# Loading K and R of the first four units two tokens to a partition

## The chip, the core and the metric

The kernel runs on one core of a Trainium2 chip. The metric is the device time of one execution in microseconds (us); the figure used for comparisons is the median of several executions. Engines are named as the profile names them: PE is the matmul side of TensorE, PEld its weight loads, DVE is VectorE, ACT is ScalarE, POOL is GpSimd, SP is SyncE (SPq is SP's queue of DMA issues).

## What is computed

An RWKV-5 attention is followed by a two-layer block. The attention has batch 4, 8 heads, 768 tokens, 48 elements a head:

```python
for t in range(S):
    kt, vt, rt = k[:, :, t], v[:, :, t], r[:, :, t]
    cur = np.einsum('bhd,bhe->bhde', u[None] * kt, vt)
    y[:, :, t] = np.einsum('bhd,bhde->bhe', rt, state + cur)
    state = w[None, :, :, None] * state + np.einsum('bhd,bhe->bhde', kt, vt)
```

The result, as x with 3072 tokens of 384 elements, goes through `h = x @ w_in` (384 to 2048), the SmeLU with beta 1 (0 below -1, h above 1, and (h + 1)**2 / 4 between), and `g @ w_out` (2048 to 384). Inputs and output are float32.

## The kernel before

**Units.** The attention is done in chunks of 128 tokens. One batch and one chunk make a unit: 24 units, numbered chunk by chunk over the four batches, so units 0 to 3 (U0 to U3) are the first chunk of the four batches and carry no state from before. Two units make a pair m (256 tokens), which is the tile of the two-layer block.

**A unit's steps** (function `attention`, lines 469 to 674). K, R and V of a unit are loaded as float32 tiles of 128 tokens x 8 heads x 48 (line 427: every token and head is one run of 192 bytes, 192 KB a load). K is multiplied by w to the power -(t+1), `Winv` (line 483), R by w to the power t, `Wpow` (line 487), where t is the token's place in the chunk; both products go as bf16 into one tile KR, each head padded from 48 to 64. TensorE transposes KR in eight blocks, two heads each (line 505), a copy brings them from PSUM to SBUF as RK (line 508; helper at line 318). Matmuls of RK with itself give the 128x128 matrices A of each head (line 535); they are masked to the strict triangle (lines 550 and 553, AT; for a few units after a cast `am` at line 546). The diagonal comes from the product P of the two halves of RK and a matmul with u (lines 565 and 571, copied as dg). Matmuls of AT with V (line 609), and from the second chunk on of RK with the state Tbd (line 606), give y; VD (line 596) is added to it (line 621) to give x. TensorE transposes x for the first six units (line 631) and a DMA does for the others (line 639), into xTa. For the state, KR's K half is the stationary operand of matmuls with V (line 657); T is updated and scaled (lines 664 to 668) and copied as bf16 into Tbd (line 672). From unit 10 on a DMA transposes KR (line 524). The squares of x at line 647 feed only a check of range at the end.

**The two-layer block.** Layer one of a pair has eight groups of six matmuls (line 715), each evicted by ACT as a square (line 730, g). The PSUM pool "h" has two slots, so a group waits for the eviction of the group two before it. Layer two of a unit has four groups of four matmuls (line 749), each of which needs one quarter of w_out. The weights come as float32 in four loads of w_in (I0 to I3) and four of w_out (O0 to O3), 768 KB each, in runs of 2048 and 1536 bytes (line 454), and are cast to bf16 by DVE, ACT and POOL (line 318).

**What sets the order.** All instructions are listed as operations with engines, dependencies, slots of pools and due times, and a planner (`Plan.run`, line 98) places them one by one with costs of its own; every engine then executes its own list in that order. The due times come from `CFG` (`due`, `step`, `bias`) and, for the early loads, from `CFG["order"]` (lines 433 to 437). All loads go through SP's queue, in one order, with at most eight DMAs under way at a time. A load also waits until a slot of its pool is free; the weights' float32 tiles have the five slots of "wf". TensorE fills its time up to a set point with dummy matmuls of zeros (line 403).

Of the kernel before, what the change touches and what calls it, by code (L numbers as in the profile page):

```python
# [9 lines left out]
F32 = mybir.dt.float32  # L10
BF16 = mybir.dt.bfloat16
AF = mybir.ActivationFunctionType
# [2 lines left out]

SEM = 0.06
CFG = {
    "order": "U0 U1 U2 U3 I0 I1 I2 I3 O0 O1 O2 U4 U5 O3 U6 U7",
    "tpe": 10,
    "dmm": 8,  # L20
    "xpe": 6,
    "pair": 4,
    "cold": 9.0,
    "fine": 0,
    "am0": 2,
    "am1": 0,
    "norm": 100.0,
    "wide": 0,
    "due": [32.65, 38.55, 28.55, 31.54, 45.68],
    "step": 9.83,  # L30
    "warm": 24.0,
    "steady": 45.0,
    "slack": 0,
    "split": 2,
    "bias": {
        "P": 2.76, "am": -14.26, "at": -12.0, "bd": -7.97, "cI": 4.41, "cO": 11.29, "c_uw": 4.37, "dc": 5.73,
        "dg": 7.99, "ku": -5.64, "kw": 7.93, "ldK": -0.11, "ldR": 0.75, "ldVf": 1.96, "mask": -7.09, "red": 3.59,
        "rk": -1.31, "rkk": 0.04, "rkr": 5.61, "rw": -4.62, "st": 7.95, "t": -0.44, "tr": 0.61, "trd": -2.94,
        "trk": -6.22, "trr": 1.71, "tw": -8.79, "v": 0.76, "vd": -0.65, "x": 1.06, "x2": 1.39, "xp": -2.11,
        "xt": 0.98, "xtd": -1.36, "y": -5.96,  # L40
    },
}

# [151 lines left out]
def pe(t):  # L195
    return {"PE": (t, t + 0.17)}
# [22 lines left out]
def kernel(  # L219
# [30 lines left out]
    while len(D_m) < NB + 2:  # L250
# [8 lines left out]
    slots = {  # L259
        "a": 4, "h": 2, "o": 2,  # L260
        "K": 6, "R": 6, "Vf": 6, "wf": 5, "KR": 4, "KU": 3, "V": 6, "RK": 4, "AT": 3, "P": 2, "VD": 3, "dg": 3,
        "x": 5, "x2": 2, "g": 5, "os": 3, "sq": 1, "ss": 2, "am": 2,
    }
    P = Plan(slots)
    rows = rot.tile([1, 2, H, DP], F32, name="rows", tag=f"g_{slots['g'] - 1}")
    lw = rot.tile([128, H, D], F32, name="lw", tag="x2_1")

    def get(b, shape, dtype):
        pl = psum if b.pool in ("a", "h", "o") else rot
        nm = f"{b.pool}_{b.slot}"  # L270
        b.t = pl.tile(shape, dtype, name=nm, tag=nm)
        return b.t
# [19 lines left out]
    i_int = const.tile([128, 1], mybir.dt.int32, name="i_int")  # L292
    i_col = const.tile([128, 1], F32, name="i_col")
    negj_col = const.tile([128, 1], F32, name="negj_col")
    Wpow = const.tile([128, H, D], F32, name="Wpow")
    Winv = const.tile([128, H, D], F32, name="Winv")
    uw = const.tile([128, NP, 2], BF16, name="uw")
# [19 lines left out]
    def copy(eng, o, i):  # L317
        (nc.scalar.copy if eng == "ACT" else V_ENG[eng].tensor_copy)(o, i)  # L318

    def pair(t, p):  # L320
        return t[:, 2 * p : 2 * p + 2, :].rearrange("q h d -> q (h d)")
# [3 lines left out]
        return bass.AP(tensor=src.tensor, offset=src.offset, ap=[[0, 1], [1, H * D]])  # L325

    heads = lambda t: t.rearrange("p (h d) -> p h d", h=H)
    c_wr = P.op("c_wr", {"SP": (0.5, 0)}, lambda e: nc.sync.dma_start(out=w_sp[0:128:64, :], in_=w.rearrange("(s h) d -> s (h d)", s=2)), due=-1000, dma=(0.05, 1, 0.5))  # L328
    c_ubc = P.op("c_ubc", {"SP": (0.4, 0)}, lambda e: nc.sync.dma_start(out=u_bc, in_=row_bcast(u)), due=D_m[CFG["dmm"] // UB] - 25, dma=(0.7, 8, 0.6))
    c_cols = P.op("c_col", {"POOL": (0.2, 0.2)}, lambda e: nc.gpsimd.iota(i_int, pattern=[[0, 1]], base=0, channel_multiplier=1), due=-100)  # L330

    def f_kr(i):
        def fn(e):
            nc.vector.memset(KR[i], 0.0)
        return fn

    kr0 = [P.op(f"c_kr{i}", {"DVE": (0.48, 0.5)}, f_kr(i), due=-90 + i) for i in range(slots["KR"])]

    def f_col(e):
        nc.vector.tensor_copy(i_col, i_int)  # L340
        nc.vector.tensor_scalar(negj_col, i_col, -1.0, -1.0, ALU.mult, ALU.add)
    c_icol = P.op("c_icol", {"DVE": (0.3, 0.35)}, f_col, deps=[c_cols], due=-92)
    c_ident = P.op("c_ident", {"POOL": (0.6, 0.7)}, lambda e: make_identity(nc, ident), due=-98)

    def f_um(e):
# [26 lines left out]
        for s in range(2):  # L372
            nc.scalar.activation(lw[:, lws[s]], wbb[s].t, AF.Ln)
    c_lw = P.op("c_lw", {"ACT": (0.58, 0.65)}, f_lw, deps=[c_wb], uses=wbb, due=-98)
    c_winv = P.op("c_winv", {"ACT": (0.5, 0.58)}, lambda e: nc.scalar.activation(Winv, lw, AF.Exp, scale=negj_col), deps=[c_lw, c_icol], due=-97)  # L375
    c_wpow = P.op("c_wpow", {"ACT": (0.5, 0.58)}, lambda e: nc.scalar.activation(Wpow, lw, AF.Exp, scale=i_col), deps=[c_lw, c_icol], due=-96)
    c_lrow = P.op("c_lrow", act(384, False), lambda e: nc.scalar.copy(rows[:, 0, :, 0:D], lw[0:1]), deps=[c_lw, c_rz], due=8.2)

    c_ur = P.op("c_ur", {"ACT": (0.4, 0)}, lambda e: nc.scalar.dma_start(out=rows[:, 1, :, 0:D], in_=heads(row(u))), deps=[c_rz], due=-99.5, dma=(0.05, 1, 0.6))
# [32 lines left out]

    loads = {}

    def add_load(i):
        b, c = units[i]
        t0 = c * C
        res = {}  # L420
        due = LD[i]
        for j, (nm, src) in enumerate((("K", k), ("R", r), ("Vf", v))):
            bf = Buf(nm)

            def fn(e, bf=bf, src=src):
                t = get(bf, [128, H, D], F32)
                nc.sync.dma_start(out=t, in_=src[b, :, t0 : t0 + C, :].rearrange("h s d -> s h d"))  # L427

            o = P.op(f"ld{nm}{i}", {"SP": (0.5, 0)}, fn, after=[loads[i - 1][nm][1] if i else None], allocs=[bf], due=due + 0.1 * j, dma=(1.08, 64, 0.6))
            res[nm] = (bf, o)  # L430
        loads[i] = res

# [10 lines left out]
    for tag, q in [(x[0], int(x[1:])) for x in ORDER if x[0] in "IO"]:  # L443
# [8 lines left out]
        def fn(e, bf=bf, src=src, shape=shape):  # L452
            t = get(bf, shape, F32)
            nc.sync.dma_start(out=t, in_=src)  # L454
# [14 lines left out]
    def attention(i):  # L469
# [4 lines left out]
        by_pe, by_mm, x_pe = i < CFG["tpe"], i < CFG["dmm"], i < CFG["xpe"]  # L474
        D0 = D_m[m] + 1.5 * j
        (Kb, Ko), (Rb, Ro), (Vb, Vo) = loads[i]["K"], loads[i]["R"], loads[i]["Vf"]
        krb, vb, rkb, atb, yb, xb = Buf("KR"), Buf("V"), Buf("RK"), Buf("AT"), Buf(A), Buf("x")
        both = {**pool(384), "DVE": (0.51, 0.56)}
        prev = state.get(b)

        def f_kw(e):
            krb.t = KR[krb.slot]
            V_ENG[e].tensor_mul(krb.t[:, H:, 0:D], Kb.t, Winv)  # L483
        o_kw = P.op(f"kw{i}", both, f_kw, deps=[Ko, c_winv] + kr0, uses=[Kb], allocs=[krb], due=D0 - 6)

        def f_rw(e):
            V_ENG[e].tensor_mul(krb.t[:, :H, 0:D], Rb.t, Wpow)  # L487
        o_rw = P.op(f"rw{i}", both if soft else {"DVE": both["DVE"]}, f_rw, deps=[Ro, c_wpow, o_kw], uses=[Rb, krb], due=D0 - 5.8)

        def f_v(e):  # L490
            get(vb, [128, H, D], BF16)
            copy(e, vb.t, Vb.t)
        o_v = P.op(f"v{i}", {**act(384, False), **({**dve(384, True), **pool(384, False)} if soft else {})}, f_v, deps=[Vo], uses=[Vb], allocs=[vb], due=D0 - 4)

        if by_pe:
            trb = Buf(A)

            fine = i < CFG["split"]

            def f_tr(e, part):  # L500
                if trb.t is None:
                    get(trb, [128, 2 * NP, 128], BF16)
                    get(rkb, [128, 2 * NP, 128], BF16)
                for p in part:
                    nc.tensor.transpose(trb.t[:, p, :], pair(krb.t, p), ident)  # L505

            def f_rk(e, part):
                copy(e, rkb.t[:, part], trb.t[:, part])

            kp, rp = slice(NP, 2 * NP), slice(0, NP)  # L510
            half = {**act(512), **dve(512, True)}
            if fine:
                o_trk = P.op(f"trk{i}", pe(0.22), lambda e: f_tr(e, range(NP, 2 * NP)), deps=[o_kw, c_ident], uses=[krb], allocs=[trb, rkb], due=D0 - 5)
                o_trr = P.op(f"trr{i}", pe(0.22), lambda e: f_tr(e, range(NP)), deps=[o_rw], uses=[krb, trb, rkb], after=[o_trk], due=D0 - 4.8)
                o_rk1 = P.op(f"rkk{i}", half, lambda e: f_rk(e, kp), deps=[o_trk], uses=[trb, rkb], due=D0 - 4.2)
                o_rk2 = P.op(f"rkr{i}", half, lambda e: f_rk(e, rp), deps=[o_trr], uses=[trb, rkb], due=D0 - 4)
                o_rk = [o_rk1, o_rk2]
            else:
                o_tr = P.op(f"tr{i}", pe(0.44), lambda e: f_tr(e, list(range(NP, 2 * NP)) + list(range(NP))), deps=[o_kw, o_rw, c_ident], uses=[krb], allocs=[trb, rkb], due=D0 - 4.8)
                o_rk = [P.op(f"rk{i}", {**act(1024), **dve(1024, True)}, lambda e: copy(e, rkb.t, trb.t), deps=[o_tr], uses=[trb, rkb], due=D0 - 4)]  # L520
        else:
            def f_trd(e):
                get(rkb, [128, 2 * NP, 128], BF16)
                nc.sync.dma_start_transpose(out=rkb.t, in_=krb.t.rearrange("p h d -> p (h d)"))
            o_rk = [P.op(f"trd{i}", {"SP": (1.35, 0)}, f_trd, deps=[o_kw, o_rw], uses=[krb], allocs=[rkb], due=D0 - 9, dma=(1.45, 64, 0.0))]
# [124 lines left out]
        if c < NCH - 1:  # L650
            stb = Buf(A)
            DS = D_m[m + 2] + 1.5 * j

            def f_st(e):
                get(stb, [128, NP, 2 * D], F32)
                for p in range(NP):
                    mm(stb.t[:, p, :], pair(krb.t[:, H:, :], p), pair(vb.t, p), start=True, stop=True)  # L657
            o_st = P.op(f"st{i}", pe(0.17), f_st, deps=[o_kw, o_v], uses=[krb, vb], allocs=[stb], due=D0 - 0.2 if c else DS - 10)

            def f_t(e):  # L660
                for s in range(2):
# [235 lines left out]
```

## Time and profile before

| what | value |
|---|---|
| median of 8 executions | 179.17 us (178.07 to 182.0) |
| the profiled execution | 180.63 us, of which the span of its instructions 178.9 us |
| mean granted TensorE clock | 0.984 |
| busy in the span: PE, DVE, ACT, POOL | 168.4, 111.8, 121.2, 99.3 us |
| layer one, 576 matmuls | 273 ns each, 77.0 us |
| layer two, 400 matmuls | 323 ns each, 77.1 us |
| dummy matmuls | 47, 10.9 us |

The profile is one execution, taken by the hardware profiler. Times in its views count from the first instruction. The chain of work that ended last is followed back from the last instruction: at each step to what released it, or to the instruction before it on its engine. Busy times of matmuls overlap by their pipelining (273 ns each, while a group of six follows the one before it by 0.65 us in the timeline), so sums of busy time on PE are above the time that passes.

### The profile page before, as it was taken

To read this page: it belongs to the slowest core of one execution; us is meant where nothing else is said; L and a number is where in the kernel's file an instruction comes from. 1 tells how busy PE (TensorE), PEld (TensorE's weight loads), DVE (VectorE), ACT (ScalarE), POOL (GpSimd) and SP (SyncE) were. 2 spreads that over 40 slices of the span, in tenths; PEclk is the share of its full clock that TensorE was granted. 3 is DMA by queue.
4 is the path that set the end of the run, shared out by engine and by line. 5 is a ranking of instruction groups with operands and counts; after the bars stand their busy time and mean duration, and the time that the engine had idled before them with its cause. 6 is when DMAs were issued, how large, how long until landed. Compare 5 with 4: busy or idle time off the path is not lost.

```text
span 178.9 us, 4529 instructions
## 1 busy us (share of the span) xinstructions
PE 168.4 (94%) x1719; PEld 127.7 (71%) x1719; DVE 111.8 (63%) x220; ACT 121.2 (68%) x267; POOL 99.3 (56%) x138
## 2 busy tenths in 40 slices
PE   7999888959999999999999999999999999999990
PEld 4777676846777777777777777777777868777770
DVE  5599895496797898948862786697674817010000
ACT  4665777784768959559775597894896864755520
POOL 8234463126769697956776359599797941300000
PEclk9999999996999999999999999999999999999997
DMA  4999999797994999899699997998989863311111
GB/s 83 190 190 344 344 377 315 150 251 153 238 198 103 195 207 188 178 159 220 118 196 174 207 211 136 196 212 156 192 154 199 169 146 93 88 51 44 46 44 49
DMA packets 104717, 31.14 MB, mean 174 GB/s; under 512 B 97778, under 2 KB 103156, under 8 KB 104692
## 3 DMA queue, kind: packets, MB, share of 16 engines
q1 hardware_dynamic: 104676, 30.81, 80.4%
q8 instruction: 14, 0.23, 0.6%
q14 instruction: 11, 0.09, 0.2%
q10 hardware_dynamic: 16, 0.00, 0.0%
HBM read 20.65 MB, written 4.72 MB: 142 GB/s over the span
## 4 chain that ended last, share of the span: by engine, by line
PE 75%; DMA 11%; SPq 7%; issue 3%; POOL 1%; ACT 0%; POOLq 0%
PE o L749 35%; PE h L715 30%; DMA wf<-in_moe_w_out_dram 6%; SPq L427 5%; DMA wf<-in_moe_w_in_dram 5%; PE a L535 3%; PE a L609 2%; PE a L606 2%; PE a L657 2%; POOL w_out_sb L318 1%; PE a L505 1%; SPq L454 1%; SPq L328 0%; PE a L631 0%; ACT os L318 0%
## 5 line engine op out<-in xcount | busy, mean ns | idle before, releaser
L749 PE MATMUL o<-w_out_sb,g 128*128 128x384 bf16 (+2 forms) x400 | 77.1, 323 | 1.5 <-POOL w_out_sb L318 1.0
L715 PE MATMUL h<-xTa,w_in_sb 128*128 128x256 bf16 x576 | 77.0, 273 | 0.2 <-ACT w_in_sb L318 0.2
L730 ACT ACTIVATE g<-h 128x512 bf16<-128x512 f32 x96 | 56.6, 595 | 29.5 <-PE h L715 28.4
L715 PEld LDWEIGHTS <-w_in_sb 128*128 128x128 bf16 x576 | 54.6, 98 | 13.6 <-ACT w_in_sb L318 0.5
L749 PEld LDWEIGHTS <-g 128*128 128x128 bf16 x400 | 37.3, 98 | 17.6 <-issue 2.3
L553 DVE TENSOR_TENSOR AT<-a,umask 128x512 bf16<-128x512 f32 x46 | 29.0, 684 | 10.0 <-PE a L535 9.9
L596 POOL TENSOR_TENSOR VD<-V,dg 128x384 f32<-128x384 bf16 x18 | 15.9, 883 | 13.4 <-ACT V L318 4.0
L586 POOL TENSOR_TENSOR KU<-KU,R 128x384 f32<-128x384 f32 x16 | 17.3, 1082 | 4.0 <-DMA R<-in_r_dram 2.9
L487 DVE TENSOR_TENSOR KR<-R,Wpow 128x384 bf16<-128x384 f32 x22 | 16.0, 729 | 3.0 <-DMA R<-in_r_dram 2.7
L585 POOL TENSOR_TENSOR KU<-K,u_bc 128x384 f32<-128x384 f32 x16 | 17.6, 1101 | 0.0
L621 DVE TENSOR_TENSOR x<-a,VD 128x384 bf16<-128x384 f32 x24 | 13.1, 553 | 4.8 <-PE a L609 4.2
L318 ACT CAST Tbd<-T 48x192 bf16<-48x192 f32 x38 | 13.2, 348 | 3.6 <-POOL T L668 2.5
L668 POOL TENSOR_TENSOR T<-T,wc 128x192 f32<-128x192 f32 x20 | 11.4, 572 | 7.1 <-DVE T L664 3.6
L483 DVE TENSOR_TENSOR KR<-K,Winv 128x384 bf16<-128x384 f32 x16 | 12.4, 777 | 3.0 <-ACT Winv L375 1.6
L318 ACT COPY os<-o 128x384 f32<-128x384 f32 (+2 forms) x21 | 9.7, 463 | 6.2 <-PE o L749 5.1
L647 ACT ACTIVATE x<-x 128x384 bf16<-128x384 bf16 x24 | 12.4, 518 | 1.5 <-DVE x L621 1.0
L664 DVE TENSOR_TENSOR T<-T,a 48x192 f32<-48x192 f32 x32 | 11.2, 349 | 3.1 <-PE a L657 2.5
L403 PE MATMUL o<-zero 128*128 128x256 bf16 x47 | 10.9, 369 | 1.1 <-DVE zero L356 1.1
L318 ACT CAST V<-Vf 128x384 bf16<-128x384 f32 x20 | 10.1, 507 | 2.0 <-DMA Vf<-in_v_dram 1.8
L591 DVE TENSOR_REDUCE dg<-KU 128x8 f32<-128x384 f32 x16 | 8.7, 546 | 4.1 <-POOL KU L586 3.9
L800 POOL TENSOR_TENSOR ss<-sq 128x256 bf16<-128x256 bf16 x8 | 6.3, 789 | 8.3 <-ACT sq L791 8.3
L483 POOL TENSOR_TENSOR KR<-K,Winv 128x384 bf16<-128x384 f32 x8 | 8.2, 1028 | 2.5 <-DMA K<-in_k_dram 2.5
(83 smaller groups left out, 169.4 us busy)
## 6 DMA issues: line engine op xcount, KB each, us to landing
K<-in_k_dram SPq DMA_DIRECT2D x24, 192.0 KB, 4.1
R<-in_r_dram SPq DMA_DIRECT2D x24, 192.0 KB, 3.8
Vf<-in_v_dram SPq DMA_DIRECT2D x24, 192.0 KB, 4.2
out_dram<-os SPq DMA_DIRECT2D x19, 192.0 KB, 3.0
wf<-in_moe_w_in_dram SPq DMA_DIRECT2D x4, 768.0 KB, 8.0
wf<-in_moe_w_out_dram SPq DMA_DIRECT2D x4, 768.0 KB, 10.1
out_dram<-os SPq DMA_DIRECT2D x8, 96.0 KB, 2.2
xTa<-x SPq DMA_TRANSPOSE x18, 2.5
```

The source lines that it names most:

```text
L318: (nc.scalar.copy if eng == "ACT" else V_ENG[eng].tensor_copy)(o, i)
L483: V_ENG[e].tensor_mul(krb.t[:, H:, 0:D], Kb.t, Winv)
L487: V_ENG[e].tensor_mul(krb.t[:, :H, 0:D], Rb.t, Wpow)
L553: nc.vector.tensor_mul(atb.t[s], at_p[s].t, umask4)
L585: nc.gpsimd.tensor_mul(kub.t, Kb.t, u3)
L586: nc.gpsimd.tensor_mul(kub.t, kub.t, Rb.t)
L596: V_ENG[e].tensor_mul(vdb.t, vb.t, dgb.t[:, :, None].to_broadcast([128, H, D]))
L621: nc.vector.tensor_add(xb.t, yb.t[:, 0:384].rearrange("p (h d) -> p h d", h=H), vdb.t)
L647: nc.scalar.activation(x2b.t, xb.t.rearrange("p h d -> p (h d)"), AF.Square, accum_out=xn[:, i : i + 1])
L715: mm(hb.t[:, f, :], w_in_sb[:, kk, c * 128 : (c + 1) * 128], xT[m][:, kk, cols], start=(kk == 0), stop=(kk == nKb - 1))
L730: nc.scalar.activation(gb[m].t[:, 2 * n : 2 * n + 2, :], hb.t, AF.Square, bias=0.5, scale=0.5)
L749: mm(ob.t[:, : hi - lo], gb[m].t[:, f, j * C : (j + 1) * C], w_out_sb[:, f, lo:hi], start=(f == 0), stop=(f == nN - 1))
```

## The change

K and R of units 0 to 3 are loaded into a tile for each pair of units, in a slot of the pool "wf": unit 0 of the pair takes partitions 0 to 63, unit 1 takes 64 to 127, and every partition holds two neighbouring tokens, so a run is 384 bytes. There are four loads for a pair, of 64 partitions and 192 KB each. V is loaded as before. The multiplies then work on even tokens (z = 0) and odd tokens (z = 1) of both units at once, with four tables W2 in place of Winv and Wpow (four more exps on ACT); Winv and Wpow remain for the units after. TensorE transposes them, eight blocks for K and eight for R of a pair, and the copies from PSUM to RK write every second column, which puts the tokens in order again. The K half, which the state's matmuls need with tokens on partitions, is transposed back from RK by TensorE (four blocks a unit) and copied to a tile KB. The KR tiles are cleared only in their padding. Beside that the planner's settings differ (order of loads, due times, biases; x of units 6 and 7 transposed by TensorE; the am cast for unit 2 too; A matmuls of both units in one operation from pair 3 on; no split of unit 0's and 1's transposes), and the order of the instructions of every engine is planned anew.

```diff
-    "order": "U0 U1 U2 U3 I0 I1 I2 I3 O0 O1 O2 U4 U5 O3 U6 U7",
+    "order": "U0 U1 U2 U3 I0 I1 I2 I3 O0 O1 U4 O2 O3 U5 U6 U7",
-    "xpe": 6,
-    "pair": 4,
+    "xpe": 8,
+    "pair": 3,
+    "duo": 2,
-    "am0": 2,
+    "am0": 3,
-    "due": [32.65, 38.55, 28.55, 31.54, 45.68],
-    "step": 9.83,
+    "due": [8.31, 25.74, 32.52, 37.4, 41.83],
+    "step": 9.95,
-    "slack": 0,
-    "split": 2,
+    "slack": 0.19,
+    "split": 0,
...
+    c_w2 = []
+    for q in range(4):
+        c_w2.append(P.op(
+            f"c_wd{q}", {"ACT": (0.5, 0.58)}, lambda e, q=q: nc.scalar.activation(W2[:, q], lw, AF.Exp, scale=i2_col[:, q : q + 1]),
+            deps=[c_lw, c_icol], due=-97 + 0.1 * q,
+        ))
...
+        if i < UB * CFG["duo"]:
+            if i % UB == 0:
+                bf = Buf("wf")
...
+                            nc.sync.dma_start(out=bf.t[x * DP : (x + 1) * DP, j], in_=src[b, :, t0 : t0 + C, :].rearrange("h (i s) d -> i h (s d)", s=2))
...
+                        src = dd["D"].t[:, q].rearrange("p h (s d) -> p h s d", s=2)[:, :, z]
+                        V_ENG[e].tensor_mul(kb.t[:, H - q * H : 2 * H - q * H, 0:D], src, W2[:, 2 * q + z])
...
+                            nc.tensor.transpose(tb.t[:, z, p, :], pair(dd["kr"][z].t, NP - q * NP + p), ident)
...
+                dst = rkb.t[:, NP - q * NP : 2 * NP - q * NP, :].rearrange("a p (i s) -> a s p i", s=2)
+                copy(e, dst, dd["tr"][q].t[:, :, :, j * DP : (j + 1) * DP])
...
+                        nc.tensor.transpose(kbp.t[:, p, :], rkb.t[:, NP + p, :], ident)
...
+                    copy(e, kbb.t.rearrange("q h d -> q (h d)"), kbp.t.rearrange("q p d -> q (p d)"))
```

## The prediction

> **What bounds the kernel now.** First the chain of work that ended last, in order of time:
>
> ```profile
> 13.74 8.24 DMA wf<-in_moe_w_in_dram
> 21.98 11.11 DMA wf<-in_moe_w_out_dram
> ...
> 33.14 0.70 POOL w_out_sb L318
> 33.83 5.09 issue
> ...
> 38.94 1.35 POOL w_out_sb L318 x2
> ...
> 40.33 1.44 PE o L749 x4
> ```
>
> Columns: start, us, what. Up to 38.9 the end hangs on transfers; from 40.33 on it is TensorE's. The group at 40.33 is the fourth of layer two (I call it L2#4), the first to need O3, the last quarter of w_out. The 5.09 of "issue" at POOL is POOL waiting for O3: it was issued at 32.97 (timeline of SP's queue), took 5.9 to land (view of line 454 in that stretch), so landed at 38.87, and was cast by 40.33: 1.46 us later. Second, the windows (us, then busy PE, PEld, DVE, ACT, POOL, clock, DMA share, GB/s):
>
> ```profile
> 5.00:10.00 5.00, 4.72 (x38) 3.51 (x38) 3.48 (x9) 2.71 (x8) 0.47 (x2) 1.00 1.35 195
> 20.00:25.00 5.00, 4.58 (x69) 3.71 (x66) 4.76 (x14) 4.22 (x8) 3.58 (x7) 1.00 1.05 381
> 30.00:35.00 5.00, 4.46 (x36) 3.33 (x35) 3.27 (x7) 3.94 (x8) 1.36 (x2) 1.00 0.86 182
> 35.00:40.00 5.00, 3.31 (x50) 2.68 (x48) 3.94 (x9) 4.27 (x10) 1.06 (x2) 1.00 0.93 242
> 40.00:45.00 5.00, 4.67 (x49) 3.18 (x49) 3.29 (x8) 2.51 (x9) 3.51 (x5) 0.66 0.81 161
> ```
>
> The queues are full from 5 us on, but with the 192-byte runs of K, R and V they move 195 GB/s, with the weights' runs (1536 and 2048 bytes) 381. TensorE falls to 3.31 of 5 us before O3 comes, and then its clock is 0.66 for a stretch: 0.34 x 5 = 1.7 us of work lost. Third, the timeline's last work on TensorE:
>
> ```profile
> 171.81 2.26 PE L749 MATMUL o<-w_out_sb,g 128*128 128x256 bf16 x27
> ```
>
> TensorE ends at 174.07; copy, store and drain take 178.9 - 174.07 = 4.8. From 45 us to there it is busy throughout. So: end = start of L2#4 + remaining matmul work + 4.8, and before that is 40.33 + 133.7 + 4.8, of which 1.7 is half clock, so 132.0 of warm work. I price the change by when L2#4 can start and how much work then remains.
>
> **What the Trainium skill says.** (1) "DMA: Bandwidth & Descriptors", Why small descriptors are slow: each run carries a fixed cost beside its bytes; 195 against 381 GB/s agrees. (2) "SBUF — State Buffer", Door 1: a transfer reaches only the ports of its partitions; 64 partitions in one half reach 8 of 16, so half of its 435 GB/s. Every load in this trace fills 128 partitions, so nothing here shows it. It matters: each new load fills 64. (3) "VectorE: DVE Perf Modes", What auto-detection actually checks: 16-bit data doubles its rate only at step ±1. The contiguous 128x512 copies of RK took 0.42 here; the new ones write with step 2. (4) "TensorE: Matmul & The Clock Gate", Part 1: an idle stretch of about 3.4 us halves the clock; here the dip at 35 to 40 and the 0.66 after it agree.
>
> **The loads.** The first ten unit loads were issued from 1.50 and landed from 4.50 to 13.96 (timeline plus time to landing): 1.05 us each, 196.6 KB at 195 GB/s being 1.01. Eight of the first twelve (K, R of units 0 to 3) become 384-byte loads, same bytes, half the packets (the built kernel's order shows them as 64x8x96, so the runs are what the change says). Low end, if only packets count: 1/195 at 192 bytes and 1/381 at some 1790 bytes give a fixed part of 0.54 ns a run over all 16 engines, and at 384 bytes 268 GB/s, so 0.73 us, with the 4% of loss seen 0.77. High end from the ports: an estimate by the skill's SBUF page, 196.6 KB / 217 GB/s = 0.90, with 4% 0.94. I take 0.85: 8 x 0.20 = 1.6 us saved; ends 0.9 and 2.2. The count of DMAs is equal (four per pair before and after), so SP's issue time is, too.
>
> **The order on SP.** Order "U4 before O2" and the due times put, by the order of instructions, only K of unit 4 before O2 and R of unit 4 before O3; before, K and R of unit 5 also stood ahead of O3. Two loads of 1.05 move behind it: 2.1 us. O3 lands at 38.87 - 1.6 - 2.1 = 35.2, L2#4 may start at 35.2 + 1.46 = 36.7. New waits on SP: I3 and O0 now wait for the two pair tiles (they take slots of the pool "wf"), freed by POOL's four multiplies of the second pair, at about 15 us (data to some 12 us, then 1.03 us each by the row of L483 on POOL); before, these two were issued at about 16 to 17, so they are just covered; uncovered, each us late is one us on O3. What is moved behind O3: K, R of unit 5 land at about 37.3 and 38.3, V of unit 5 at 42.5 (41.1 before). TensorE reaches unit 5's transposes about 2.6 us after L2#4, at 39.4, and its output matmuls at 44.4, by the order of instructions and the rows' durations, so both are in time by about one us.
>
> **ACT and DVE.** ACT gets four exps for the pair factors (0.6 each, as Winv) ahead of everything, while Winv and Wpow move behind the first copies: by ACT's order unit 0's second RK copy ends near 11.5, where TensorE began the first A matmuls at 9.75; some 1.8 us late. The first layer-one group comes at about 19.5, as before (19.42), since the loss is partly won back by earlier weights (I0 lands at 16.24 - 1.6 = 14.6). Then ACT from the first cast to the twelfth g, which TensorE's 14th layer-one group needs for its PSUM slot and which L2#4 stands behind: 12 g x 0.60 = 7.2, four RK copies 2.4, four squares x 0.71 = 2.8, six Tbd 2.2, two T pairs 1.3, two weight casts to w_in 1.2, one to w_out 0.5, KB copy 0.55, am 0.55, xTa 0.48, four dg 0.6: 19.8 us. From 14.6 that is 34.4, plus 0.65 and 0.25 for the 14th group and an A group 35.3 without a gap. With 1.5 us of gaps 36.8. DVE: KB copy and strided RK copies cost 0.42 to 0.68 instead of 0.42; eight at most 2.1, while the KR clears shrink by about as much earlier; DVE was at 4.76 of 5 in 20 to 25, so that cover is thin, and I count its excess in the gaps. On TensorE, 16 transposes back (KB): 2 x 0.61 = 1.2 us, all ahead of the first layer-two group, where it still fills time with dummy matmuls (47 before, 40 after by the order): nothing; if that cover is gone, 1.2. Units 6 and 7 transpose x on TensorE: six more, 0.66 by its rows, at the dense end of the road, plus copies that ACT and DVE have room for.
>
> **The sum.** L2#4 starts at 36.8, 3.5 earlier. But less is done by then. By the order, left over compared with before: two layer-one groups 1.3, eight transposes 0.6, eight A 0.4, four dg 0.24, six x transposes 0.66: 3.2 as rows, 2.4 if small matmuls overlap; 2.8. TensorE no longer idles for three us, so I expect no half clock. End: 36.8 + 132.0 + 2.8 + 4.8 = 176.4, against 178.9: 2.5 us less. The profiled execution took 180.63, 1.7 around its span, and the median is 179.17, 1.46 below it; I subtract the same 2.5: **176.7 us**. One per cent (1.8 us) is about what a measurement of this kernel tells from no change.
>
> **Rivals.**
> - *Packets alone count and ACT has no gaps* (10%): L2#4 at 35.3, end 1.5 earlier: 175.2.
> - *ACT takes the place of the transfers* (14%): 19.8 us on ACT at 85% busy take 23.3, L2#4 at 38.8: 2.0 later, 178.7. For it: ACT was only 14.4 of 20 busy in 15 to 35; its instructions rarely run without waits. Against: its additions sit early, beside transfers.
> - *The half clock stays* (11%): any dip before L2#4 costs 1.7: 178.4.
> - *Late K, R, V of units 5 to 7* (5%): TensorE waits some 1.5 at 40 to 48: 178.2.
> - *The 64-partition loads are slower, not faster* (10%), the other side: if halving the ports halves even today's 195 GB/s, a load takes 2.0, eight cost 7.6 more; O3 at 38.87 - 2.1 + 7.6 = 44.4, end 44.4 + 1.5 + 132.0 + 2.8 + 4.8 = 185.5 of span, 185.8. It decides from 1.23 us a load (no gain) and 1.45 (slower by 1%). Against it: a packet's time is mostly fixed at this size, and 0.94 is the ports' own price.
>
> **How the numbers follow.** Forecast 50%, own range 175.6 to 177.9. Faster by over 1% is below 177.4: four fifths of the forecast (0.41), the first rival (0.10), a little of the middle ones (0.04): 0.55. Slower: the last (0.10) and tails: 0.12. Within 1%: 0.33. Range 174.9 to 180.2: it leaves out the last rival and some of the first.
>
> **What would show it.** Landing spacing of the pair loads 0.77 to 0.94; O3 landed near 35; first L749 group that waits for O3 near 37; PEclk without a 6 near slice 9; TensorE ending near 171.6. I am wrong if the spacing is above 1.05, if the twelfth g ends after 37, or if TensorE stands between 40 and 48.

## The result, and the profile after

| | before | after |
|---|---|---|
| median, same chip | 179.96 us (48 executions) | 183.01 us (17 executions) |
| the profiled execution | 180.63 us, span 178.9 | 182.43 us, span 180.7 |
| fourth layer-two group (L2#4) starts | 40.33 | 37.41 in the chain (first matmul 37.34) |
| TensorE busy from there, gaps left out | 133.7 (1.7 of it lost to the half clock) | 135.6 |
| gaps of TensorE over 0.15 us, 42 to 172 us | none | 3.4 us in four |
| TensorE ends | 174.1 | 176.4 |

The changed kernel is slower by 1.2%: ratio 1.012, 95% interval 1.0081 to 1.0159. (Disturbed executions are left out of that ratio, so it is not the quotient of the two medians.) The forecast was 176.7 us, 1.4% faster.

The windows of the changed kernel, with the same columns as those of before (us, then busy PE, PEld, DVE, ACT, POOL, clock, DMA share, GB/s):

```profile
5.00:10.00 5.00, 3.91 (x28) 2.74 (x27) 1.59 (x3) 3.19 (x7) 2.21 (x5) 1.00 1.33 194
...
35.00:40.00 5.00, 5.00 (x65) 3.91 (x64) 4.08 (x8) 2.77 (x7) 2.90 (x5) 1.00 0.90 176
40.00:45.00 5.00, 4.98 (x58) 3.47 (x56) 4.67 (x11) 3.09 (x7) 2.81 (x5) 1.00 0.83 160
```

The hole at 35 to 40 (3.31 of 5) is filled and the clock keeps 1.00 after it: from 35 to 45 us the profile is as forecast. But in the first row TensorE has less to do (3.91; before, 4.72), and the queues there move 194 GB/s, as with the old loads. The chain of waits of the changed kernel:

```profile
21.10 0.36 DVE xTa L322
...
22.24 10.90 DMA wf<-in_moe_w_out_dram
...
33.19 1.28 POOL w_out_sb L322 x2
...
34.51 0.81 PE o L849 x4
...
37.08 0.33 PE a L618 x8
37.41 0.76 PE o L849 x4
```

Layer two is now line 849, layer one 815. The transfer in it is O2, no longer O3; from 34.51 on TensorE goes from work to work, and L2#4 at 37.41 waits for nothing. O3 was issued at 28.05 and landed at 36.15. The first layer-one group starts at 21.73, right after the copy xTa at 21.10; before it was 19.42. The loss shows in the waits of TensorE from 40 to 172 us (what waited, for what, us in total, times, longest); the same view of before, from 42 on, is empty:

```profile
PE h L815 <- ACT g L830: 2.3, 1, 2.3
PE o L849 <- ACT g L830: 0.8, 2, 0.6
```

And here is the stop itself, first TensorE's timeline (start, duration, idle before and what ended it in brackets), then ACT's:

```profile
123.72 0.50 PE L849 MATMUL o<-w_out_sb,g 128*128 128x384 bf16 x2 [0.58 <-ACT g L830]
...
124.44 0.82 PE L815 MATMUL h<-xTa,w_in_sb 128*128 128x256 bf16 x6
127.59 0.81 PE L815 MATMUL h<-xTa,w_in_sb 128*128 128x256 bf16 x6 [2.34 <-ACT g L830]
```

```profile
122.66 0.51 ACT L322 CAST V<-Vf 128x384 bf16<-128x384 f32 x1 [1.54 <-DMA Vf<-in_v_dram]
123.08 0.59 ACT L830 ACTIVATE g<-h 128x512 bf16<-128x512 f32 x1
123.57 0.83 ACT L891 ACTIVATE sq<-w_in_sb 128x768 bf16<-128x768 bf16 x1
124.30 0.70 ACT L322 CAST Tbd<-T 48x192 bf16<-48x192 f32 x2
125.31 0.51 ACT L322 CAST V<-Vf 128x384 bf16<-128x384 f32 x1 [0.31 <-DMA Vf<-in_v_dram]
125.72 0.71 ACT L322 CAST Tbd<-T 48x192 bf16<-48x192 f32 x2
126.44 0.52 ACT L730 ACTIVATE x<-x 128x384 bf16<-128x384 bf16 x1
126.87 0.19 ACT L730 ACTIVATION_READ_ACCUMULATOR x<-x 128x1 f32 x1
126.96 1.07 ACT L830 ACTIVATE g<-h 128x512 bf16<-128x512 f32 x2
```

The wait is "for g", but the g is not slow (about 0.6 us). Between the g at 123.08 and the next at 126.96 ACT works off a square of weights, four Tbd copies, a V and a square of x. That V waits 0.31 us for its transfer, and another V, ahead of the g at 123.08, has waited 1.54 us. "TensorE waits for ACT's g" therefore has two possible roots: the order on ACT, or the lateness of V. The chain has V in it:

```profile
118.90 0.35 SPq L722
...
119.30 0.57 SPq L464
...
119.92 1.61 SPq L464
...
121.57 3.71 DMA Vf<-in_v_dram
...
125.31 0.51 ACT V L322
```

SP had issued the loads of the two V only at 119.30 and 121.57, behind two transposes of x (line 722).

### The profile page after: what moved, and what is told of

Read it like the earlier page. It is cut to its first block, busy times and chain, and to the rows that moved or that the text cites. A ratio compares the mean times of both kernels' runs of the same rounds, so it can differ in the third digit from the quotient of the medians.

```text
span 180.7 us, 4566 instructions
## 1 busy us (share of the span) xinstructions
PE 168.8 (93%) x1734; PEld 127.6 (71%) x1734; DVE 109.4 (61%) x219; ACT 122.1 (68%) x271; POOL 112.6 (62%) x155
## 3 DMA queue, kind: packets, MB, share of 16 engines
HBM read 20.65 MB, written 4.72 MB: 140 GB/s over the span
## 4 chain that ended last, share of the span: by engine, by line
PE 63%; DMA 17%; POOL 5%; SPq 5%; ACT 4%; DVE 2%; issue 1%; POOLq 0%; DVEq 0%
PE o L849 27%; PE h L815 24%; DMA Vf<-in_v_dram 9%; DMA wf<-in_moe_w_out_dram 6%; SPq L464 3%; PE a L618 3%; PE a L692 2%; DMA R<-in_r_dram 2%; PE a L588 2%; SPq L448 1%; PE a L757 1%; PE a L689 1%; POOL KU L669 1%; PE a L547 1%; POOL VD L679 1%
## 5 line engine op out<-in xcount | busy, mean ns | idle before, releaser
L849 PEld LDWEIGHTS <-g 128*128 128x128 bf16 x400 | 36.7, 98 | 16.7 <-ACT g L830 1.6
L636 DVE TENSOR_TENSOR AT<-a,umask 128x512 bf16<-128x512 f32 x45 | 28.2, 683 | 9.2 <-PE a L618 9.0
L679 POOL TENSOR_TENSOR VD<-V,dg 128x384 f32<-128x384 bf16 x18 | 16.6, 925 | 6.2 <-ACT V L322 3.4
L768 POOL TENSOR_TENSOR T<-T,wc 128x192 f32<-128x192 f32 x20 | 13.0, 655 | 5.2 <-DVE T L764 3.0
L322 ACT CAST V<-Vf 128x384 bf16<-128x384 f32 x18 | 9.2, 511 | 6.7 <-DMA Vf<-in_v_dram 6.6
L322 ACT CAST Tbd<-T 48x192 bf16<-48x192 f32 x36 | 12.5, 347 | 1.7 <-PE a L689 1.1
L555 POOL TENSOR_TENSOR KR<-K,Winv 128x384 bf16<-128x384 f32 x10 | 10.0, 999 | 4.6 <-DMA R<-in_r_dram 2.8
L420 PE MATMUL o<-zero 128*128 128x256 bf16 x40 | 9.5, 392 | 1.1 <-DVE zero L367 1.1
L555 DVE TENSOR_TENSOR KR<-K,Winv 128x384 bf16<-128x384 f32 x10 | 8.5, 855 | 2.7 <-DMA K<-in_k_dram 2.7
L692 PE MATMUL a<-V,AT 128*128 128x48 bf16 x192 | 8.8, 186 | 0.4 <-ACT dg L322 0.4
```

Source lines behind the costliest of these rows:

```text
L636: nc.vector.tensor_mul(atb.t[s], at_p[s].t, umask4)
L679: V_ENG[e].tensor_mul(vdb.t, vb.t, dgb.t[:, :, None].to_broadcast([128, H, D]))
L768: o_t = P.op(f"tw{i}", pool(192), lambda e: nc.gpsimd.tensor_mul(T[b], T[b], wc3), deps=[o_t, c_wc], due=DS - 7)
L849: mm(ob.t[:, : hi - lo], gb[m].t[:, f, j * C : (j + 1) * C], w_out_sb[:, f, lo:hi], start=(f == 0), stop=(f == nN - 1))
```

## The experiments

Each run is compared with the kernel before on the same chip. The number after "Measured" is the ratio of the two times (above 1 is slower), with its 95% interval in brackets; the changed kernel itself is at 1.012. The places of stops are those of the run's one profiled execution. Unless a diff says otherwise, all other instructions keep their order. Orders are changed after planning, by moving named operations of the list `todo` ahead of others.

**e1_early_v: V of two late units issued ahead of a transpose.**

```diff
+    for name, ahead in (('ldVf20', 'xtd16'), ('ldVf21', 'xtd16'),):
```

> The changed kernel with one difference: on SP the V loads of units 20 and 21 are issued ahead of the two x transposes of units 16 and 17 that stood before them; every other instruction keeps its place. Theory (the late V loads hold ACT's queue, and g behind it, so TensorE stands 3.1 us between 122 and 128): L815's wait for g near 127 (2.3 us) goes, TensorE's busy time between 122 and 128 rises from 3.1 to 5.5 or more of 6, the time falls by 2 to 3 us against the changed kernel (183.0), to about 180.5. Rival (the late part has too much to do on ACT and POOL in this order whatever V does): the stall comes a few us later, the gain is below 1 us.

Measured: 1.0165 (1.0114 to 1.0216). ACT no longer waits for these V, and yet TensorE stops for 1.57 us at 124.57, and for 2.23 us at 136.74. So V of these two units being late is not the whole cause: 1.57 us remain with no wait on ACT in front of them, and a new stop appears where ACT waits 3.50 us for an output buffer still being stored, followed by a lower clock (0.94 from 130 to 160 us). As the rival said, there was no gain.

**e2_spread: the pair tile over all partitions.** Unit x of a pair goes to partitions x, x + 2, ..; the copies then take every second column as source.

```diff
-                            nc.sync.dma_start(out=bf.t[x * DP : (x + 1) * DP, j], in_=src[b, :, t0 : t0 + C, :].rearrange("h (i s) d -> i h (s d)", s=2))
+                            nc.sync.dma_start(out=bf.t[x:128:2, j], in_=src[b, :, t0 : t0 + C, :].rearrange("h (i s) d -> i h (s d)", s=2))
...
-                copy(e, dst, dd["tr"][q].t[:, :, :, j * DP : (j + 1) * DP])
+                copy(e, dst, dd["tr"][q].t[:, :, :, j:128:2])
```

> The changed kernel, but the two units of a pair take even and odd partitions of the tile in place of its lower and upper half, so that each 64-partition load reaches partitions all over the memory; runs stay 384 bytes, copies pick every second column, order and costs of the plan are the same. Theory (the ports of one half of the partitions held the 384-byte loads at about 200 GB/s): pair loads land 0.75 to 0.85 us apart, about 260 GB/s, the first quarter of w_in lands near 14.3 in place of 16.17, the fourth layer-two group starts up to 1.5 us before 37.34. Rival (a 384-byte run costs what two 192-byte runs cost, wherever it lands): landing times stay within 0.3 us.

Measured: median 183.79 us against 181.0 (six executions, no interval, so the time decides nothing). The packets did go faster: from 10 to 11 us 661 packets of 384 bytes took 22 ns each (the median) and the queues moved 254 GB/s, where the changed kernel had 528 at 39 ns and 203 GB/s. But the last R of the second pair landed at 13.23 instead of 14.09, a step of 0.96 us a load and not the 0.75 to 0.85 expected, and the first quarter of w_in at 15.8, not 14.3. L2#4 started at 36.23, 1.1 us ahead of the changed kernel, and TensorE kept that lead until 120 us. Then it stopped for 0.94 us at 122.10 and 2.06 us at 124.57, again for g, its clock fell to 0.89 and 0.94 in the two stretches from 120 to 140 us, and it ended at 176.7, no earlier than the changed kernel (176.4). In this execution the faster start did not reach the end.

**e3_order_alone: before, with O3 ahead of K of unit 5.** No new loads.

```diff
+    for name, ahead in (('ldO3', 'ldK5'),):
```

> The kernel before with one difference: the last quarter of w_out is issued on SP ahead of K and R of unit 5 (before: behind). Theory (this order, not the longer runs, gave the changed kernel its earlier fourth layer-two group): that quarter lands 2 us earlier, near 36.8, the group starts near 38.3 in place of 40.33, and the half clock at 40 to 43.5 goes or moves; the time falls by 1 to 2 us if unit 5 stays in time. Rival (the longer runs gave it): landing moves by less than 1 us.

Measured: 0.9991 (0.996 to 1.0022), no change. O3 landed at 35.63 instead of 38.87, but L2#4 started at 40.15 in the chain, where before it was 40.33. The chain of that kernel shows why:

```profile
29.65 6.53 DMA K<-in_k_dram
...
36.20 0.84 DVE KR L483
...
38.44 1.20 DVE AT L553 x2
...
39.76 0.40 PE a L535 x8
40.15 0.76 PE o L749 x4
```

Eight A matmuls of unit 5 stand ahead of L2#4 on TensorE, and they wait for VectorE's work on K of unit 5. The edit itself made that K late: it landed at 34.3 before and lands at 36.18 here, behind O3, and these matmuls start at 39.76 instead of 38.94. So the edit exchanged the wait for O3 for another that ends 0.2 us earlier. The run shows that SP's order moves O3 by 3.2 us; what an earlier L2#4 is worth it does not show, as there was none.

**e4_settings_alone: the changed planner settings with the old loads** (`"duo": 0`, and no W2 tables).

> The changed kernel with the pair tiles off: all units loaded as before, none of the four extra exps, no transposes back; settings (order, due times, biases) stay those of the change, and the plan is made anew. Theory (the pair tiles bring nothing, the settings lose in the late part): within 1.5 us of the changed kernel. Rival (the pair tiles' extra work is the loss): at or below the kernel before, 180 or less.

Measured: 1.0069 (1.0026 to 1.0112). So a good half of the loss (0.7 of 1.2 points) is there without the new loads, though the intervals overlap and the plan, made anew, is not quite that of the changed kernel. TensorE's longer gaps there: 1.00 us at 112.09, for a V that stands on ACT behind an output copy waiting 0.89 us for its buffer, and 0.39 us at 126.74, for g. The gain at the start is there without the new loads too. O3 was issued at 27.89 and took 8.0 us to land, so 35.9 (changed: 36.15), and L2#4 starts as early as with them (37.34), here in the chain:

```profile
37.28 0.81 PE o L849 x4
```

**e5_after_long and e6_before_long: shorter late transfers.** K, R and V of units 12 on are read as 1536-byte runs; the tiles then hold other tokens' data.

```diff
+                if i < 12:
...
+                else:
+                    flat = src[b].rearrange("h s d -> (h s d)")[c * C * H * D : (c + 1) * C * H * D]
+                    nc.sync.dma_start(out=t.rearrange("p h d -> p (h d)"), in_=flat.rearrange("(p f) -> p f", p=128))
```

> The changed kernel with K, R and V of units 12 to 23 read as 128 runs of 1536 bytes each, one for each partition, instead of 1024 runs of 192 bytes: same bytes, same count of DMAs, same order, other tokens' data in the tiles (so what those units compute is not the reference's). Theory A, the transfers of the late units absorb the lead: their queue time falls by about half, TensorE has no gap above 0.5 us between 100 and 140 us, and the lead of 3 us at the fourth layer-two group reaches the end: 2 to 3.5 us below the changed kernel, so 0.99 to 1.00 of the kernel before. Rival B, the order of work on ACT, or GpSimd's load, stops TensorE: gaps of 2 us or more stay between 112 and 130, and the time stays at 1.01 of the kernel before.

> The kernel before with the same edit (K, R and V of units 12 to 23 as 1536-byte runs; other tokens' data). Theory A and B alike: TensorE is busy from 40 us to the end there already, so faster late transfers change nothing: 0.995 to 1.005. If it gains 1% or more, the late transfers cost the kernel before too, in a way that its trace does not show, and the pair of this and the changed kernel with the same edit must be compared with each other: A expects the changed one to be 1 to 2 us the faster of the two, B 1 to 2 us the slower.

Measured: changed 1.0052 (1.0022 to 1.0083), before 0.9956 (0.9924 to 0.9989). Faster late transfers help both, by 0.7 and 0.4 points. That is less than the loss; in the changed kernel the stop stays, shorter:

```profile
PE h L819 <- ACT g L834: 1.6, 1, 1.6
```

ACT waits for no V in front of it. It is as long as the stop that e1_early_v left (1.57 us): the share of ACT's order.

**e7_after_pool and e8_before_pool: less work for GpSimd, late.**

```diff
-            get(ssb, [128, 256], BF16)
...
-            nc.gpsimd.tensor_add(ssb.t, sqb.t[:, 0, :], sqb.t[:, 1, :])
-            nc.gpsimd.tensor_add(ssb.t, ssb.t, sqb.t[:, 2, :])
-            nc.gpsimd.tensor_add(mx[n // 2], ssb.t[:, 0:128], ssb.t[:, 128:256])
+            nc.gpsimd.tensor_add(mx[n // 2], sqb.t[:, 0, 0:128], sqb.t[:, 0, 128:256])
```

> The changed kernel with one of the three adds of each of the eight squared-weight reductions on GpSimd (0.43 us kept, 0.74 and 0.67 left out: 11 us of GpSimd's work between 100 and 145 us; part of the column-norm test is left out). The order of all else stays. Theory C, GpSimd, busy 3.4 to 3.9 of 4 us from 104 on, is the late limit: the gaps of TensorE between 112 and 130 fall below 0.5 us in sum and the time by 2 to 3 us, to 0.995 to 1.00 of the kernel before. Theory A (transfers) or B (ACT's order) expect gaps of 2 us or more to stay and 1.01.

> The kernel before with the same adds left out on GpSimd. All theories: TensorE had no gap there, so 0.995 to 1.005; a gain of 1% would say that GpSimd's late load costs the kernel before as well.

Measured: 1.0123 (1.0059 to 1.0187) and 0.999 (0.9955 to 1.0024). GpSimd, busy 3.4 to 3.9 of 4 us in that stretch, is not the cause: the stop is 2.06 us with 11 us of its work gone.

**e9_g_first: g ahead of other work on ACT.**

```diff
+    for name, ahead in (('v21', 'x2_19'), ('x2_18', 'e14_0'), ('sq4', 'sq12'), ('ss4', 'sq12'),):
```

> The changed kernel with four operations moved back in the order: on ACT the cast of V of unit 21, the square of x of unit 18 and one square of weights (0.51 + 0.71 + 0.83 us), which stand between the two squares g of layer one where TensorE stopped for 2.34 us, go behind those g; the weight square and its three adds on GpSimd some 20 us further back. Everything is still computed. Theory B, ACT's order in the late part loses the lead: the 2.34 us gap falls below 0.5 us, TensorE's gaps between 40 and 172 us to about 1.2 in sum, and the time by some 2 us, to 0.996 to 1.003 of the kernel before. Rival A, the late transfers hold the pace: the gap opens again at the next V or at a later place, 1.007 to 1.012.

Measured: 1.0167 (1.0099 to 1.0235), no faster than the changed kernel. The stop at 125 fell from 2.34 to 0.61 us, nearly as theory B said. Then TensorE stopped further down, for 2.27 us at 137.27, behind this on ACT:

```profile
132.76 0.51 ACT L322 CAST V<-Vf 128x384 bf16<-128x384 f32 x1 [1.92 <-DMA Vf<-in_v_dram]
...
137.78 0.48 ACT L322 COPY os<-o 128x384 f32<-128x384 f32 x1 [3.52 <-DMA out_dram<-os]
138.15 0.85 ACT L891 ACTIVATE sq<-w_in_sb 128x768 bf16<-128x768 bf16 x1
138.90 1.08 ACT L830 ACTIVATE g<-h 128x512 bf16<-128x512 f32 x2
```

The same stop stands in e1_early_v (2.23 us at 136.74, ACT waiting 3.50 us), so it is not one execution's. Theory B alone falls: with ACT's order mended at one place, a transfer that comes late holds ACT at the next.

**e10_before_bunch: such a bunch put into the kernel before.**

```diff
+    for name, ahead in (('x2_17', 'g8_3'), ('sq8', 'g8_3'),):
```

> The kernel before with two of ACT's operations moved, nothing else: the square of x of unit 17 (0.71 us) back and a square of weights (0.83 us) forward, so that between two squares g near 127 us ACT has 4.8 us of other work instead of 3.3, while TensorE has 2.6 to 3.3 us of work there. Theory B: TensorE stops there for 1 to 2 us and the time grows by as much, 1.005 to 1.012. Rival A: no gap over 0.4 us and 0.997 to 1.003.

Measured: 1.0004 (0.9958 to 1.005). The profile has the stop in the place where it was put: TensorE waits 1.39 us for g at 133.8, while ACT works off two Tbd pairs, an output copy, three squares of x and the square of weights with no wait over 0.15 us between them. So a bunch on ACT is enough for a stop. The median does not show it; the interval holds both no change and the lower end of the expectation, and the profiled execution also has a gap of 2.03 us at 98.98, for a transposing DMA (RK), far ahead of the edit. As a measure of time the run is inconclusive.

**e11_spread_g_first and e12_g_first_early_v: e9_g_first with e2_spread, and with e1_early_v.**

> The changed kernel with both the pair tiles spread over all partitions (unit x of a pair on partitions x, x+2, ..) and the reordered ACT operations of the run e9_g_first. Theory B: the 1.1 us by which the spread tile led the changed kernel up to 120 us now reaches the end, so 1 us below e9_g_first: 0.988 to 0.998 of the kernel before, the first version that beats it. Rival A: a wait on V or R of units 20 to 23 takes it again: the same time as e9_g_first within 0.4 us.

> The changed kernel with the reordered ACT operations of e9_g_first and, as in e1_early_v, V of units 20 and 21 issued ahead of a transpose of x on the sync queue. Theory B with a late V on top: the remaining gap of 0.58 us at 123 us, where ACT waits 1.54 us for V of unit 20, goes as well; 0 to 0.6 us below e9_g_first. Rival: the second stall of e1_early_v, 2.2 us near 137 us behind an output copy that waits for its buffer, stays: 1 to 2 us above e9_g_first.

Measured: 1.0197 (1.0124 to 1.027) and 1.0181 (1.0114 to 1.0247). Both missed. The first stops 2.37 us at 124.0 and 1.19 us at 142.36, the second 1.50 us at 136.32, where ACT waits 2.26 us for a V and 2.79 us for an output buffer. The rival of e12_g_first_early_v, that the second stop of e1_early_v stays, holds for the stop, though the time is only 0.1 points above e9_g_first and not 1 to 2 us.

**e13_long_g_first: shorter late transfers and the ACT order of e9_g_first, at once.**

> The changed kernel with both edits at once: K, R and V of units 12 to 23 as 1536-byte runs (other tokens' data), and the ACT operations of e9_g_first moved behind the squares g. Theory AB, late transfers and ACT's order act together: TensorE's gaps after 60 us fall below 0.6 us in sum, the end is 2 to 3.3 us earlier than the changed kernel's, 0.992 to 0.998 of the kernel before, and below e5_after_long (1.005) by about 1.5 us. Rival D, something else holds the late pace (a wait of about the same size opens in another place): 1.004 or more.

Measured: 1.0008 (0.9985 to 1.0032), against 1.012 for the changed kernel, 1.0052 for the transfers alone and 1.0167 for the order alone. TensorE's waits for g shrink to this:

```profile
PE h L819 <- ACT g L834: 1.4, 2, 0.8
```

The larger of the two is at 149.11, where the moved square of weights now stands next to another and waits 1.52 us for GpSimd: the edit's own. So the two causes act together: transfers alone gave 0.7 points, the order alone nothing, both 1.1. The sum of TensorE's stops agrees for the most part, 3.4 us in the changed kernel, 2.3 in e5_after_long and 1.9 here; the 1.55 us between the first and the last are 0.9 points. But the ratio stopped at 1.001, above the 0.992 to 0.998 expected, while before with the same transfers (e6_before_long) is at 0.996. With its stops cut to 1.9 us in sum the changed kernel is still not the faster one.

**e14_g_first_store_early and e16_spread_store_early: e9_g_first, e16 with e2_spread too, and the late store and a V ahead of a waiting transpose.**

```diff
+    for name, ahead in (('v21', 'x2_19'), ('x2_18', 'e14_0'), ('sq4', 'sq12'), ('ss4', 'sq12'), ('out12_1', 'trd20'), ('out12_0', 'trd20'), ('ldVf22', 'trd20'),):
```

> e9_g_first with the two half stores of unit 12 and V of unit 22 issued on the sync queue ahead of a transpose of RK that waits there (all data as in the changed kernel). In e9_g_first ACT stood 3.5 us near 137 us behind an output copy whose buffer waited for that store, and TensorE 2.3. Theory AB, queue order: the 137 us stop goes, 1.5 to 2.5 us below e9_g_first (1.017), about 1.005. Theory A in its strict form (the total of late transfers): the next transfer is late instead, 1.012 to 1.018.

> e14_g_first_store_early with the pair tiles spread over all partitions, which gave 1.1 us more lead up to 120 us in e2_spread. Theory AB: 0.5 to 1.1 us below e14_g_first_store_early. Theory A strict: the same as e14_g_first_store_early within 0.4 us. To beat the kernel before it would need 0.99.

Measured: 1.0129 (1.0083 to 1.0175) and 1.0126 (1.0063 to 1.0189). The 2.27 us at 137 are gone in both, but e14 stops 1.83 us at 123.61 and five more times for 0.3 to 0.8 us, and e16 in seven places for 0.2 to 0.8 us. That is what theory A in its strict form expected (1.012 to 1.018, and no difference between the two): the next transfer is late instead. Before the 1.83 us in e14 ACT waits 2.79 us for a V. Neither beats the kernel before.

**e15_order_long: e3_order_alone with the late transfers of e6_before_long.**

> The kernel before with the last quarter of w_out loaded ahead of K and R of unit 5 (as e3_order_alone, 0.999) and K, R and V of units 12 to 23 as 1536-byte runs (as e6_before_long, 0.996; other tokens' data). Theory AB: the lead of 1.4 to 1.7 us that e3_order_alone had at 42 us and lost by 104 us now reaches the end: 0.985 to 0.990. Rival D: the lead is lost for another reason: 0.994 to 0.998.

Measured: 0.9959 (0.9932 to 0.9986), the same as e6_before_long (0.9956). Theory AB missed, and rival D's number came. But there was no lead that could have been carried: L2#4 starts at 40.76 in its profile, not before the 40.48 of e6_before_long, again behind unit 5's A matmuls. The "lead of 1.4 to 1.7 us" that the expectation takes from e3_order_alone goes back at least in part to the half clock (1.7 us) that before's profiled execution had and that of e3_order_alone had not. So this run does not tell whether a lead would reach the end.

## Why the prediction was wrong

| term of the sum, in the profiled execution | forecast | measured | difference |
|---|---|---|---|
| start of L2#4 | 36.8 | 37.3 | +0.5 |
| warm work of TensorE from there | 132.0 + 2.8 | 135.6 | +0.8 |
| stops of TensorE from there | 0 | 3.5 | +3.5 |
| from TensorE's end to the end of the span | 4.8 | 4.3 | -0.5 |
| span | 176.4 | 180.7 | +4.3 |

**The loads: mis-sized.** Forecast 1.6 us saved over eight loads, at 0.85 a load. The last R of the second pair was issued at 8.89 and took this long to land:

```profile
L448 SPq DMA_DIRECT2D wf<-in_r_dram x1: 633/633/633, 8.9 to 8.9; - x1
...
DMA to landing us min/median/max: 5.2/5.2/5.2
```

So it landed at 14.09. From the first landing (5.01) to there are nine steps of 1.01 us (two of the ten loads are V). That is beyond the 0.94 of the high end, and just below the 1.05 of before, above which the prediction calls itself wrong. With the first load landing at 5.01 instead of 4.50, the tenth came no earlier than before (13.96), and I0 landed at 16.17, where it had landed at 16.24: the gain was next to nothing. e4_settings_alone, with the old loads, has O3 and L2#4 as early as the changed kernel. The Trainium skill's "SBUF — State Buffer", Door 1, says that partitions 0 to 63 reach only half of the ports, an estimated 217 GB/s. The trace agrees: with 384-byte packets the queues of the changed kernel move 203 GB/s from 10 to 11 us, and 254 when e2_spread gives every load all ports. The rival that halving the ports would halve today's rate did not come: 1.01 is well below the 1.23 from which it would have decided.

**The order on SP: right in kind, too small.** O3 landed at 36.15, 2.7 us earlier, where the forecast gave 2.1 to the order and 1.6 to the loads; e3_order_alone gives 3.2 to the order alone, e4_settings_alone 3.0 with the old loads. The order gave all of it.

**ACT and DVE: the first part wrong.** The first layer-one group was forecast "at about 19.5, as before" and came at 21.73. The earlier I0 that was to win the 1.8 us back did not come, GpSimd needed 12.25 to 16.65 for the four multiplies of the second pair, and six RK copies on ACT between 8 and 24 us took 0.75 each where the forecast counted four at 0.60. The strided copy on DVE cost 0.73 instead of 0.42. The forecast's 0.42 to 0.68 was a little too low. Nevertheless L2#4 started at 37.3, half a us behind the forecast; "ACT takes the place of the transfers" (38.8) did not happen. That the start came so near is in part luck: loads that gave nothing and a late start of layer one stood against an order that gave a us more than forecast.

**The half clock: gone at 40 us, but priced from one execution, and it came back elsewhere.** The prediction takes the dip for an idle stretch of some three us and says that the trace agrees with the 3.4 us of the Trainium skill. It does not: ahead of it TensorE stopped twice, for 1.02 us at 37.91 and 1.00 us at 39.34, with work between. Nor does such a hole bring the half clock each time. e8_before_pool has before's order up to there, two stops of 1.03 and 0.90 us, and a clock that stays at 1.00:

```profile
35.00:40.00 5.00, 3.07 (x47) 2.47 (x45) 4.37 (x9) 4.23 (x10) 1.47 (x3) 1.00 0.99 257
40.00:45.00 5.00, 5.00 (x69) 3.71 (x68) 3.93 (x11) 3.41 (x12) 4.45 (x6) 1.00 0.90 174
```

Of the six profiles of before and its variants two show the dip, before and e15_order_long. These two executions have a mean clock of 0.984 and 0.985, the four without it 0.995 or more. The record of the experiments lists the mean clock of 147 executions of before: 37 have 0.988 or less, and on each of four chips these are longer than the others, by 0.3 to 1.2 us on average. So, as an estimate from these figures (a quarter of the executions, about 1 us each), the term is worth some 0.3 us in the mean, and the forecast took the whole 1.7 off the median. The Trainium skill's "TensorE: Matmul & The Clock Gate", Part 1, says that the window in which activity is counted runs free of the kernel's start, so that one kernel measures differently from run to run; that only some of these profiles show the dip agrees.

The changed kernel has half clocks of its own. Seven of its 19 executions with a listed clock have 0.972 or less, lower than any of the 147 of before. Its own profile has no dip, so where theirs are is not shown. But of the eight profiles with its early order (its own, e1, e5, e7, e9, e12, e13, e14) four, e7, e9, e13 and e14, have one between 10 and 20 us, as here in e13_long_g_first:

```profile
10.00:15.00 5.00, 2.78 (x29) 1.90 (x27) 4.17 (x7) 3.58 (x9) 3.29 (x4) 0.64 1.20 259
15.00:20.00 5.00, 4.47 (x60) 4.14 (x60) 4.95 (x10) 3.44 (x8) 3.87 (x6) 0.68 1.13 304
```

TensorE has less to do from 5 to 15 us than before (7.8 of 10 us in the changed kernel, before 9.4). This early dip costs little: L2#4 starts at 37.2 to 37.7 in the four, and at 37.34 in the changed kernel's own profile. A late one costs more. After the stops of 2.23, 2.06 and 2.27 us in e1, e7 and e9 the clock fell too (e1: 0.94 from 130 to 160 us; e7: 0.89 and 0.94 from 120 to 140; e9: 0.91 from 140 to 160), which is about 1.7 us of work each, as an estimate from these means. After the 2.34 us in the changed kernel's profile it did not. So a stop can cost more than its length.

In e8_before_pool L2#4 starts at 39.89 and TensorE ends at 172.5. The changed kernel without its stops would end at 37.3 + 135.6 = 172.9. So against an execution of before without the dip the early part gains nothing at all: L2#4 is 2.6 us earlier, and 3.0 us more work stand behind it (the forecast had 2.8). This fits e13_long_g_first, which stays at 1.001.

**The failed step of the sum.** It is the assumption taken over from the trace of before, "From 45 us to there it is busy throughout", as if it held for any order: 3.5 of the 4.8 us by which TensorE ended later than the forecast's 171.6 are stops behind ACT. Before was dense because its own order made it so. The new order puts 3.5 us of ACT's other work (0.83 + 0.70 + 0.51 + 0.71 + 0.71, all rows of ACT's timeline above) between two g, while TensorE had about 1.5 us of matmuls left there (123.72 to 125.25). The order of instructions, which was at hand, shows that bunch; I read it only up to 45 us.

The second term that failed is the 1.7 us of half clock, of which the mean of before's executions holds some 0.3 by the estimate above.

The shown causes of the stops are two: ACT's order (1.57 us where ACT waits for nothing: e1_early_v, e5_after_long) and transfers that SP issues late (the rest; e5_after_long, e9_g_first). That the two together carry the difference from 1.012 to 1.001 is shown by e13_long_g_first.

Not shown is what would remain with no stop at all, why the new plan makes these bunches, and whether filling TensorE's hole at 35 to 40 in before by order alone (moving the casts of O3 and L2#4 ahead of unit 5's A matmuls) would be carried to the end: two runs of that, e17_order_pe and e18_order_pe_long, have no result. No version of this study that computes everything was faster than the kernel before by more than its interval.

**The rivals.** None of the five named this outcome. The range reached to 180.2 and "slower" had 0.12, nearly all of it put on slow loads; a new stop late in the kernel was not among the cases.

## What to carry to other kernels

When a change makes a planner reorder the whole program, the dense part of the old trace is no evidence for the new one. Between two evictions that TensorE needs, add up ACT's other work in the new order by the old rows' durations and compare it with TensorE's own work there; where ACT has more, a stop is to be expected. A lead won early is worth only what is less to do from then on: compare the work left, not only the start. And a term that comes from one execution (here the half clock) belongs into the sum with the share of executions that have it.

## What was not expected of the hardware

- With 384-byte runs, loads into 64 neighbouring partitions took 39 ns a packet and loads spread over all partitions 22 ns (medians from 10 to 11 us), but the spacing of the loads only fell from 1.01 to 0.96 us.
- Stops of TensorE far shorter than the 3.4 us that the prediction names can be followed by a half clock, and need not be. Two stops of 1.02 and 1.00 us, 0.4 us of work apart, were followed by a half clock in the profile of before; stops of 1.03 and 0.90 us at the same place in e8_before_pool were not.
- Reading half of K, R and V in long runs, 72,461 packets instead of 104,717, gave the kernel before only 0.4%, though its main queue is 80% busy over the span (73% with the long runs).
- In every timeline here ACT works its list in order, so transfers that TensorE does not itself wait for stop TensorE too: 3.52 us in which an output copy on ACT waited for its buffer cost 2.27 us of TensorE in e9_g_first, because two g stood behind that copy.
